# Neighbourhood attention on one core: mask set-up issued earlier, ScalarE's last stores issued one per tick, a border wait undeclared, and matmuls added to the last step

## The chip, the cores and the metric

The kernel runs on one NeuronCore of a Trainium2 chip. The metric is the device time of one execution in microseconds, smaller is better. The engines are TensorE (PE, with its weight loads as PEld), VectorE (DVE), ScalarE (ACT), GpSimd (POOL) and SyncE (SP). Each has its own instruction stream and runs it in order. SP only issues DMAs here. ACT and POOL issue DMAs too, between their other instructions.

## The reference

The image is 224 x 224 with 192 channels. Each pixel attends to 49 pixels: a 7 x 7 window of dilation 2, shifted inwards at the image's edges.

```
qkv = x @ wqkv                       # q, k, v: 224 x 224 x 192 each
r0 = clip(row - 6, 0, 211); c0 = clip(col - 6, 0, 211)
neighbours of a pixel: rows r0 + 0,2,..,12 and columns c0 + 0,2,..,12
logits = (q . k_neighbour) * 192**-0.5
o = softmax(logits) @ v_neighbours
out = o @ wo
```

All inputs are bfloat16.

## The kernel before, in words

Dilation 2 splits the image by row parity `rc` and column parity `cc`; within one parity the window is a dense 7 x 7. The queries are never formed as such: `aw` holds scale * wq * wk^T, so that `pg` = x * aw is compared with the raw image rows (the keys are copies of `x`), and `WP` holds wv * wo, so that `vw` = x * WP is already the projected value. A column of ones in `vw` gives the softmax's denominator.

The work is a list of 28 **steps** `(rc, j)`: (0,0), (1,1), (0,1), (1,2), ..., (1,13), (1,14), (0,13). A step is a strip of query rows of one row parity. It has 7 **ticks** (`i` from 6 down to 0); a tick handles four blocks of keys:

- `s_stage`: PE computes scores into one of two banks (`s_83`, `s_84`, L428), ACT writes their exponentials to `p_sb` (L431).
- `attend`, two ticks later: `v_stage` multiplies `p_sb` with `vw` into two accumulating banks (`y_85`, `y_86`, L448). `out_stage` takes a finished bank: DVE's reciprocal `rs` (L502) and product `o_sb` (L503), then stores (`store`, L466 and L468). In step (1,14) the products go to `oall` and leave in strided stores too (L515).
- Between them, units of the next step's work: `pv` = keys * WP (L279), evicted to `vw` by DVE and ACT in halves (L290); `pg` = keys * aw (L368), evicted by ACT to `ga`, or to `hs`, which POOL copies to `gb` (L385). `edge_item` and `place_edges` do the same for the image's left and right border (`pe`, `ge`, L347). POOL copies key blocks for the step after next (`make_keys`, L254).

The score's mask is part of the matmul. Free rows of the key tiles `xb` hold one-hot patterns (`onehot_cols`, `onehot_rows`, L164 and L170), and the same rows of the query tiles `gb` hold mask values (`mask_cols`, `mask_rows`, L149 and L154). DVE makes `xb_90`'s and `gb_102`'s; the other buffers get theirs partly from POOL and partly by SBUF-to-SBUF DMAs on SP (`spread_masks`, `spread_onehots`, L159 and L179). In buffer numbers of the profile, `XB[0..3]` are `xb_90` to `xb_93` and `GB[0..5]` are `gb_98` to `gb_103`.

The **border tile**: in the first tick of each step the last key block also reaches 6 image columns beyond the accumulators. Their sums go to `T.border`, 48 partitions in the second bank of the `pv` tile whose first bank holds a `vw` unit (`spare`). DVE's reciprocal `rse` (L487) and product `oe` (L489) read it. The instructions that evict the `vw` unit, DVE's and ACT's, are passed along as `readers`.

`load_xt` (L71) fetches a strip of the image with a transposing DMA on SP. `o_sb` has six buffers for the single tiles and two for the double tile of tick `i == 0`. Instructions run on each engine in the order in which the code emits them; waits come from tile dependencies, which are kept per buffer.

Of the kernel before, what the change touches and what calls it, by code (L numbers as in the profile page):

```python
# [31 lines left out]
def kernel(  # L32
# [147 lines left out]

    onehot_cols(0, nc.vector.tensor_copy)
# [7 lines left out]
    def warm(n):  # L189

        for _ in range(n):
            nc.tensor.matmul(y_bank[1][:].rearrange("p c e -> p (c e)"), lhsT=zero[:, 0:128], rhs=zero[:], start=True, stop=True,  # L192
                             skip_group_check=True)
# [206 lines left out]
    class Tick:  # L400
        border = None

# [31 lines left out]
    def v_stage(T, spare):  # L434


        for pos, (cc, n) in enumerate(T.pos):
# [3 lines left out]
            if not (cc == 0 and n == NT - 1):  # L441
                h, sl = 64 * ((n + 1) % 2), ((n + 1) // 2) % 2
                if n == NT - 1:
                    tile_, readers = spare or (ps_go.tile([128, 2, 2, 256], F32, name="pv", tag="go"), [])
                    T.border = tile_[0:48, 1, 0, 0:C + 1]
                parts.insert(0, (T.p[:, pos, 64:112], T.border if n == NT - 1 else y_bank[sl][h:h + 48, cc, 0:C + 1], n == NT - 1))
            for (l, o, st) in parts:
                mm = nc.tensor.matmul(o, lhsT=l, rhs=rhs, start=st, stop=True, skip_group_check=True)  # L448
# [23 lines left out]
    qn = [0]  # L472

    def out_stage(T):
# [10 lines left out]
        if i == NQ - 1:  # L485
            rs = work.tile([48, 1], F32, name="rse", tag="rse", bufs=2)
            nc.vector.reciprocal(out=rs[:], in_=T.border[:, C:C + 1])  # L487
# [11 lines left out]
        for t in range(t0, t1):  # L499
# [8 lines left out]
            if t == 0:  # L508
                for p in pieces:
                    store(pick(nc.sync), lambda d: op[d, 3:13, :], of, 6, 16, p)  # L510
                    store(pick(nc.gpsimd), lambda d: oc[d, 0:6, :], o[:, t - t0, 0], 0, 6, p)
        if last and i in (0, NQ // 2):
            ta, tb = (1, NQ // 2 + 1) if i == 0 else (NQ // 2 + 1, NQ)
            for (r0, _, d0, _) in pieces:
                pick(None).dma_start(out=op[d0, 16 * ta - 3:16 * tb - 3, :].rearrange("(t c) e -> c t e", c=16),  # L515
                                     in_=oall[r0::8, ta:tb].rearrange("p n t c -> p n (t c)"))
# [18 lines left out]
    onehot_rows(1, nc.gpsimd.tensor_copy)  # L535
# [4 lines left out]
    load_xt(2)  # L540
    both = (nc.vector, nc.gpsimd)
# [10 lines left out]
    for si, (rc, j) in enumerate(steps):  # L552
# [10 lines left out]
        for ti, i in enumerate(range(NQ - 1, -1, -1)):  # L563
# [12 lines left out]
            if si == 0 and ti == 0:  # L576
                mask_rows(3, 2, nc.gpsimd.tensor_copy)
# [66 lines left out]
```

## Time and profile before

| what | value |
|---|---|
| time, median of 3 runs | 348.85 us (348.04 to 350.31) |
| profiled execution | 346.11 us, its span 344.3 us |
| mean granted clock of TensorE | 0.967 |
| busy: PE, PEld | 303.1 us (88%), 275.6 us (80%) |
| busy: DVE, ACT, POOL | 263.9 us (77%), 253.3 us (74%), 236.3 us (69%) |
| DMA | 43.79 MB, mean 127 GB/s |

The span runs from the first to the last instruction of the profiled execution; 1.8 us of that execution lie outside it. No engine is busy throughout, so the shares do not name a bound. The view of idle time by releaser (who waited for whom) and the chain of work that ended last do that, stage by stage.

### The profile page before, as it was taken

The numbers are of one execution on the slowest core, as the hardware profiler recorded it, in microseconds if no ns is written. First come the engines' busy times: TensorE is split into PE (matmuls) and PEld (weight loads), VectorE is DVE, ScalarE is ACT, GpSimd is POOL, SyncE is SP. The second block draws the span as 40 slices with busy tenths as digits, with TensorE's granted clock in tenths as the row PEclk, the third lists the DMA queues.
The fourth block names the chain that finished last, engine by engine and source line by source line (L and its number), as shares of the span: only waits on it lengthen the run. The fifth ranks groups of instructions, "written<-read, shape, count | busy, mean of one in ns | idle before, by whom it ended". The sixth has DMA issues, their size and how long they took to land.

```text
span 344.3 us, 17618 instructions
## 1 busy us (share of the span) xinstructions
PE 303.1 (88%) x7488; PEld 275.6 (80%) x7488; DVE 263.9 (77%) x609; ACT 253.3 (74%) x424; POOL 236.3 (69%) x501
## 2 busy tenths in 40 slices
PE   7876797699999998999999999998998999988853
PEld 2455697688999997899998889897998899887842
DVE  7636987478887887878888778886787877888733
ACT  4335776677888877888888888887887888778820
POOL 5444539956997775977767977678775787861960
PEclk9688999999999999999999999999999999999976
DMA  8971445984949668294663847539385294222123
GB/s 195 208 166 33 102 119 131 169 203 109 183 113 160 149 145 155 73 187 118 111 166 90 188 106 162 131 77 199 89 187 102 74 186 118 64 78 53 46 55 86
DMA packets 112409, 43.79 MB, mean 127 GB/s; under 512 B 86984, under 2 KB 111874, under 8 KB 112330
## 3 DMA queue, kind: packets, MB, share of 16 engines
q1 hardware_dynamic: 109370, 41.00, 55.2%
q0 software_dynamic: 2368, 1.35, 2.0%
q8 instruction: 58, 0.95, 1.2%
q10 hardware_dynamic: 592, 0.31, 0.4%
q14 instruction: 21, 0.17, 0.2%
HBM read 0.29 MB, written 19.35 MB: 57 GB/s over the span
## 4 chain that ended last, share of the span: by engine, by line
PE 55%; DVE 23%; issue 9%; ACT 6%; DMA 3%; POOL 1%; ACTq 1%; SPq 0%; DVEq 0%; POOLq 0%
PE pv L279 14%; PE y_85 L448 11%; PE pg L368 10%; DVE o_sb L503 9%; DVE vw L290 6%; PE y_86 L448 5%; PE s_83 L428 5%; PE s_84 L428 4%; DMA out_dram<-o_sb 3%; DVE rs L502 3%; PE y_86 L192 2%; ACT p_sb L431 2%; ACT vw L290 2%; PE pe L322 2%; ACT hs L372 1%
## 5 line engine op out<-in xcount | busy, mean ns | idle before, releaser
L290 DVE CAST vw<-pv 64x768 bf16<-64x768 f32 (+1 forms) x112 | 95.6, 854 | 12.3 <-PE pv L279 5.2
L448 PEld LDWEIGHTS <-p_sb 128*64 128x64 bf16 (+1 forms) x1540 | 79.1, 107 | 25.7 <-issue 22.3
L290 ACT CAST vw<-pv 64x768 bf16<-64x768 f32 (+1 forms) x112 | 79.7, 712 | 27.0 <-PE pv L279 20.3
L448 PE MATMUL y_85<-vw,p_sb 128*64 128x193 bf16 (+1 forms) x840 | 85.9, 249 | 12.6 <-DVE o_sb L503 9.7
L448 PE MATMUL y_86<-vw,p_sb 128*64 128x193 bf16 (+1 forms) x672 | 82.3, 252 | 3.8 <-DVE o_sb L503 2.5
L368 PE MATMUL pg<-xt,aw 128*64 128x106 bf16 (+3 forms) x1008 | 81.6, 289 | 2.6 <-DVE vw L290 1.5
L503 DVE TENSOR_TENSOR o_sb<-y_85,rs 128x384 bf16<-128x384 f32 x108 | 60.2, 558 | 4.6 <-DMA out_dram<-o_sb 0.9
L431 ACT ACTIVATE p_sb<-s_84 128x448 bf16<-128x448 f32 x98 | 53.5, 546 | 7.3 <-DMA out_dram<-oall 5.6
L431 ACT ACTIVATE p_sb<-s_83 128x448 bf16<-128x448 f32 x98 | 53.6, 547 | 5.3 <-PE s_83 L428 4.3
L368 PEld LDWEIGHTS <-aw 128*64 128x64 bf16 x1008 | 52.5, 111 | 5.6 <-DVE vw L290 1.9
L466 POOL DMA_DIRECT2D out_dram<-o_sb x26 | 15.0, 578 | 60.4 <-DVE rs L502 60.4
L428 PEld LDWEIGHTS <-xa_87 128*64 128x64 bf16 x532 | 46.6, 112 | 4.6 <-issue 3.9
L503 DVE TENSOR_TENSOR o_sb<-y_86,rs 128x384 bf16<-128x384 f32 x81 | 45.1, 557 | 6.1 <-DMA out_dram<-o_sb 3.4
L428 PEld LDWEIGHTS <-xa_88 128*64 128x64 bf16 x532 | 47.4, 111 | 1.1 <-issue 0.6
L428 PEld LDWEIGHTS <-xa_89 128*64 128x64 bf16 x476 | 41.6, 110 | 0.4
L428 PEld LDWEIGHTS <-xb_90 128*64 128x64 bf16 x420 | 34.2, 113 | 2.4 <-issue 1.9
L428 PEld LDWEIGHTS <-xb_91 128*64 128x64 bf16 x420 | 35.3, 112 | 0.2
L502 DVE RECIPROCAL rs<-y_86 128x2 f32<-128x2 f32 x84 | 14.0, 167 | 25.7 <-PE y_86 L448 25.7
L372 ACT CAST hs<-pg 128x848 bf16<-128x848 f32 x27 | 23.4, 866 | 11.5 <-PE pg L368 10.6
L279 PE MATMUL pv<-WP,xa_87 128*64 128x192 bf16 x280 | 30.0, 253 | 1.6 <-ACT vw L285 0.5
L428 PEld LDWEIGHTS <-xb_92 128*64 128x64 bf16 x364 | 29.7, 110 | 0.5
L279 PE MATMUL pv<-WP,xa_88 128*64 128x192 bf16 x280 | 28.5, 247 | 1.0 <-DVE vw L290 0.5
(169 smaller groups left out, 1020.4 us busy)
## 6 DMA issues: line engine op xcount, KB each, us to landing
out_dram<-o_sb SPq DMA_DIRECT2D x162, 96.0 KB
out_dram<-o_sb SPq DMA_DIRECT2D x27, 60.0 KB
out_dram<-oe POOLq DMA_DIRECT2D x26, 18.0 KB, 2.7
out_dram<-o_sb POOLq DMA_DIRECT2D x26, 18.0 KB, 3.1
xb_92<-xb_90 SPq DMA_DIRECT2D x4, 112.0 KB
xb_93<-xb_91 SPq DMA_DIRECT2D x4, 112.0 KB
out_dram<-oall POOLq DMA_DIRECT2D x9, 36.0 KB, 1.8
xt<-in_x_dram SPq DMA_TRANSPOSE x15
```

Of the source, the lines that this page charges most:

```text
L192: nc.tensor.matmul(y_bank[1][:].rearrange("p c e -> p (c e)"), lhsT=zero[:, 0:128], rhs=zero[:], start=True, stop=True, skip_group_check=True)
L279: nc.tensor.matmul(pv[h:h + 64, (n - n0) // 2, (n - n0) % 2, 0:C], lhsT=keys(k, rc, cc, kt)[:, n, :], rhs=WP[:, cc, kt, :], start=(kt == 0 ...
L290: ins.append(eng(out=VW[hs, rc, cc, n0:n1, 0:C], in_=pv[hs].rearrange("p a b c -> p (a b) c")[:, 0:n1 - n0, 0:C]))
L322: nc.tensor.matmul(pg[64 * h:64 * h + 64, g // 2, g % 2, par], lhsT=AW[w][:, 64 * h:64 * h + 64], rhs=r, start=(i == 0), stop=(i == 1))
L368: nc.tensor.matmul(pr[64 * h:64 * h + 64, g, a_ - 4 * g:b_ - 4 * g, :], lhsT=AW[w][:, 64 * h:64 * h + 64], rhs=xt[b][:, k, l, 3:S - 3], st ...
L372: return eng(out=dst[:, 6:S].rearrange("p s (g r) -> p s g r", r=4), in_=pr[ps].rearrange("p g r s -> p s g r"))
L428: nc.tensor.matmul(o[h:h + 64, s0:s1, rs], lhsT=keys(k, rc, cc, kt)[:, n, :], rhs=(A, Bt)[kt][:, cc, CW * n + s0:CW * n + s1, rs], start=( ...
L431: nc.scalar.activation(out=T.p[:].rearrange("p a b -> p (a b)"), in_=ps[:, 0:4 * QW * BR], func=ACTF.Exp)
L448: mm = nc.tensor.matmul(o, lhsT=l, rhs=rhs, start=st, stop=True, skip_group_check=True)
L466: q.dma_start(out=dst, in_=src[8 * s0:8 * s1])
L502: nc.vector.reciprocal(out=rs[:], in_=y[:, :, C:C + 1])
L503: nc.vector.tensor_tensor(out=o[:, t - t0], in0=y[:, :, 0:C], in1=rs[:].to_broadcast([128, 2, C]), op=ALU.mult)
```

## The change

Four things change.

1. **Prologue and first steps.** POOL's `mask_rows(3, 2)`, `mask_rows(2, 1)` and `onehot_rows(1)` are emitted before DVE's part of the masks, ahead of everything else POOL does after its iotas. The spreads that steps 0 and 1 issued on SP between the stores are issued after the third image load. `load_xt(3)` is issued in the first tick of step 1 and not in the third.
2. **ACT's late stores.** A store that falls to ACT while ticks are still pending goes into `held`; one is taken from it at the end of each tick.
3. **The border tile.** The readers of the other bank were declared independent of the border's matmul already. Now DVE's reciprocal and product on the border are declared independent of `readers[1:]`, which is ACT's eviction.
4. **The last step.** Two matmuls of 128 x 512 on zeros follow each of its seven ticks, into a tile of the `go` pool.

```diff
+    mask_rows(3, 2, nc.gpsimd.tensor_copy)
+    mask_rows(2, 1, nc.gpsimd.tensor_copy)
+    onehot_rows(1, nc.gpsimd.tensor_copy)
     onehot_cols(0, nc.vector.tensor_copy)
     onehot_rows(0, nc.vector.tensor_copy)
     mask_cols(4, nc.vector.tensor_copy)
...
-    def warm(n):
+    def warm(n, bank=None):
+        bank = bank or y_bank[1][:].rearrange("p c e -> p (c e)")
         for _ in range(n):
-            nc.tensor.matmul(y_bank[1][:].rearrange("p c e -> p (c e)"), lhsT=zero[:, 0:128], rhs=zero[:], start=True, stop=True,
-                             skip_group_check=True)
+            nc.tensor.matmul(bank, lhsT=zero[:, 0:128], rhs=zero[:], start=True, stop=True, skip_group_check=True)
...
     class Tick:
         border = None
+        readers = ()
+
+        def apart(self, op, first=0):
+            for rd in self.readers[first:]:
+                tc.declare_no_dep(op.ins, rd.ins, reason="they are in the other bank of the tile")
...
                 if o is T.border:
-                    for rd in readers:
-                        tc.declare_no_dep(mm.ins, rd.ins, reason="they are in the other bank of the tile")
+                    T.apart(mm)
...
+    held = []
+
+    def put_off(q, issue, *args):
+
+        if q is nc.scalar and pend:
+            held.append(lambda: issue(q, *args))
+        else:
+            issue(q, *args)
...
-            nc.vector.reciprocal(out=rs[:], in_=T.border[:, C:C + 1])
+            T.apart(nc.vector.reciprocal(out=rs[:], in_=T.border[:, C:C + 1]), 1)
...
-            nc.vector.tensor_tensor(out=o[:], in0=T.border[:, 0:C], in1=rs[:].to_broadcast([48, C]), op=ALU.mult)
+            T.apart(nc.vector.tensor_tensor(out=o[:], in0=T.border[:, 0:C], in1=rs[:].to_broadcast([48, C]), op=ALU.mult), 1)
             for p in pieces:
-                store(pick(nc.gpsimd), lambda d: oc[d, W - 6:W, :], o, 0, 6, p)
+                put_off(pick(nc.gpsimd), store, lambda d: oc[d, W - 6:W, :], o, 0, 6, p)
...
     load_xt(2)
+    spread_masks(1, 3, 64)
+    spread_onehots(2)
+    spread_masks(2, 4, 32)
+    spread_onehots(3)
+    spread_masks(0, 2, 64)
+    spread_masks(5, 4, 32)
...
             if si == 0 and ti == 3:
                 make_keys(1, 0, *both)
-                spread_masks(1, 3, 64)
-                spread_masks(2, 4, 32)
-                spread_onehots(2)
-                spread_onehots(3)
-                mask_rows(2, 1, nc.gpsimd.tensor_copy)
-            if si == 1 and ti == 1:
-                spread_masks(0, 2, 64)
-                spread_masks(5, 4, 32)
...
-            if si == 1 and ti == 2 or si > 1 and rc == 0 and ti == 0:
+            if ti == 0 and (si == 1 or si > 1 and rc == 0):
                 load_xt(j + 2 + (rc == 0))
             pend.append(T)
+            if held:
+                held.pop(0)()
+            if si == len(steps) - 1:
+                warm(2, ps_go.tile([128, 512], F32, name="idle", tag="go")[:])
         assert not v_q and not q_q, (si, len(v_q), len(q_q))
-    attend(1)
-    attend(1)
+    while pend:
+        attend(1)
+    while held:
+        held.pop(0)()
```

The other stores of `out_stage` go through `put_off` in the same way. On DVE and on PE up to the last step the order of instructions is the same; of the waits there, the reciprocal `rse` loses the one for ACT. Three places move.

**POOL in the prologue.** In the program before, after the last iota, POOL clears two parts of `WP`, sets the ones of `vw`, places the first edges (eight rows, two shown) and then makes the one-hot rows and mask rows of step 1.

```order
L137 IOTA rwi 32x2
L229 MEMSET WP 64x192
L230 MEMSET WP 64x192
L245 MEMSET vw 128x14 x4
L347 COPY ga_95<-ge 128x6x7
L347 COPY gb_102<-ge 64x6x7
```

After the change, at the same place:

```order
L137 IOTA rwi 32x2
L154 COPY gb_101<-rm 32x944 x2
L154 COPY gb_100<-rm 32x944 x2
L170 COPY xb_91<-t_r 32x896 x2
L232 MEMSET WP 64x192
L233 MEMSET WP 64x192
L248 MEMSET vw 128x14 x4
L350 COPY ga_95<-ge 128x6x7
```

Six copies have moved ahead of the memsets and the edges; they stand no longer behind the edges (four of them) or behind the key copies of tick 3 (the two on `gb_100`).

**SP in steps 0 and 1.** Before, the spreads stand behind stores of step 0, and the last four stand behind all of them, just ahead of the fourth image load:

```order
L466 DMA out_dram<-o_sb 16x8x384
L468 DMA out_dram<-o_sb 16x384
L159 DMA gb_98<-gb_100 64x944 x2
L159 DMA gb_103<-gb_102 32x944 x2
L71 DMA_TRANSPOSE xt<-in_x_dram 128x3x1792
L466 DMA out_dram<-o_sb 16x8x384 x5
L71 DMA_TRANSPOSE xt<-in_x_dram 128x3x1792
```

After, the piece between the third and the fourth image load begins with all sixteen spreads and no store; the fourth load then stands ahead of the last four stores of step 0:

```order
L71 DMA_TRANSPOSE xt<-in_x_dram 128x3x1792
L159 DMA gb_99<-gb_101 64x944 x2
L179 DMA xb_92<-xb_90 64x896 x4
L159 DMA gb_100<-gb_102 32x944 x2
L179 DMA xb_93<-xb_91 64x896 x4
L159 DMA gb_98<-gb_100 64x944 x2
L159 DMA gb_103<-gb_102 32x944 x2
L473 DMA out_dram<-o_sb 16x8x384
L475 DMA out_dram<-o_sb 16x384
```

**ACT in the last step.** Before, four stores of step (1,14) stand between the exponentials of its second and third tick:

```order
L431 ACTIVATE p_sb<-s_83 128x448
L468 DMA out_dram<-oall 10x384
L468 DMA out_dram<-oall 6x192
L468 DMA out_dram<-oall 10x384
L515 DMA out_dram<-oall 16x3x384
L431 ACTIVATE p_sb<-s_84 128x448
L466 DMA out_dram<-oe 6x8x192
L431 ACTIVATE p_sb<-s_83 128x448
```

After, each exponential is followed by one store:

```order
L439 ACTIVATE p_sb<-s_83 128x448
L475 DMA out_dram<-oall 10x384
L439 ACTIVATE p_sb<-s_84 128x448
L475 DMA out_dram<-oall 6x192
L439 ACTIVATE p_sb<-s_83 128x448
L475 DMA out_dram<-oall 10x384
L439 ACTIVATE p_sb<-s_84 128x448
L530 DMA out_dram<-oall 16x3x384
L439 ACTIVATE p_sb<-s_83 128x448
L473 DMA out_dram<-oe 6x8x192
```

One store, not four, stands ahead of the third exponential.

More of the change, by code (lines that the diff above doesn't have):

```diff
@@ L443, in v_stage @@
                 if n == NT - 1:
-                    tile_, readers = spare or (ps_go.tile([128, 2, 2, 256], F32, name="pv", tag="go"), [])
+                    tile_, T.readers = spare or (ps_go.tile([128, 2, 2, 256], F32, name="pv", tag="go"), [])
                     T.border = tile_[0:48, 1, 0, 0:C + 1]
@@ L514, in out_stage @@
             for (r0, _, d0, _) in pieces:
-                pick(None).dma_start(out=op[d0, 16 * ta - 3:16 * tb - 3, :].rearrange("(t c) e -> c t e", c=16),
-                                     in_=oall[r0::8, ta:tb].rearrange("p n t c -> p n (t c)"))
+                put_off(pick(None), lambda q, ta, tb, r0, d0: q.dma_start(
+                    out=op[d0, 16 * ta - 3:16 * tb - 3, :].rearrange("(t c) e -> c t e", c=16),
+                    in_=oall[r0::8, ta:tb].rearrange("p n t c -> p n (t c)")), ta, tb, r0, d0)
     steps = [(0, 0)]
```

6 lines of the change are left out of this document (2 added, 4 removed).

## The prediction

> **What bounds the kernel now.** I read the page first for the span, then the view of idle time by releaser, and then the timeline and the table of stretches at the places where a part of the change bites. From the waits:
>
> ```profile
> span 344.3 us, 17618 instructions
> PE y_85 L448 <- DVE o_sb L503: 9.7, 28, 0.8
> DVE rse L487 <- ACT vw L290: 7.4, 14, 0.7
> ACT p_sb L431 <- DMA out_dram<-oall: 5.6, 1, 5.6
> DVE o_sb L503 <- DMA out_dram<-o_sb: 4.3, 4, 2.2
> PE s_84 L428 <- ACT p_sb L431: 3.5, 1, 3.5
> ```
>
> Columns: total us, times, longest. No engine is the bound alone. PE and DVE wait for one another: PE may not add to a y bank until DVE has read it, DVE may not read until PE has finished it. A delay on DVE inside that loop is paid by PE. Three of these rows are delays that come from outside the loop: DVE waits for ACT at the border (7.4 us), DVE waits for stores to leave its buffers (4.3 us), and ACT's exponential waits behind stores (5.6 us, of which PE feels 3.5). The change touches each.
>
> **The change part by part**
>
> *Border wait.* One instance, in the timeline:
>
> ```profile
> 115.64 0.54 DVE L290 CAST vw<-pv 64x384 bf16<-64x384 f32 x1
> 116.24 0.47 ACT L290 CAST vw<-pv 64x384 bf16<-64x384 f32 x1
> 116.74 0.16 DVE L487 RECIPROCAL rse<-pv 48x1 f32<-48x1 f32 x1 [0.56 <-ACT vw L290]
> 118.01 0.24 PE L448 MATMUL y_85<-vw,p_sb 128*64 128x193 bf16 x1 [0.43 <-DVE o_sb L503]
> ...
> 62.91 0.24 PE L448 MATMUL y_85<-vw,p_sb 128*64 128x193 bf16 x1 [0.43 <-DVE o_sb L503]
> ...
> 288.02 0.24 PE L448 MATMUL y_85<-vw,p_sb 128*64 128x193 bf16 x1 [0.42 <-DVE o_sb L503]
> ```
>
> DVE ends its own eviction at 116.18 and stands 0.56 us until ACT has evicted the other half, of a bank that the border isn't in. The product that frees y_85 follows, and PE sits 0.43 us for it. The last two rows are the first and the last of twelve such places, all with 0.42 to 0.44 us (steps 2, 3, 6, 7, 10, 11, 14, 15, 18, 19, 22, 23); elsewhere DVE comes to the border late anyway. The reciprocal keeps its wait for PE, which had written the border by then (the PE row ends 1 us earlier). So 0.56 us of DVE goes and PE gets its 0.43 us; what PE does next (the `pv` unit) finds its buffers free. 12 x 0.425 = **5.1 us**. Bounds: 0, if something else is late there by as much, and 14 x 0.53 = 7.4 us, DVE's whole idle time.
>
> *Spreads and the fourth load on SP.*
>
> ```profile
> 19.85 5.46 SPq L71 DMA_TRANSPOSE xt<-in_x_dram  x1
> ...
> 53.93 1.17 SPq L159 DMA_DIRECT2D gb_98<-gb_100  x2
> 56.42 6.69 SPq L71 DMA_TRANSPOSE xt<-in_x_dram  x1
> 63.21 3.65 SPq L466 DMA_DIRECT2D out_dram<-o_sb  x5
> 66.95 5.42 SPq L71 DMA_TRANSPOSE xt<-in_x_dram  x1
> ...
> 65.58 0.56 DVE L503 TENSOR_TENSOR o_sb<-y_86,rs 128x384 bf16<-128x384 f32 x1 [2.19 <-DMA out_dram<-o_sb]
> ...
> 61.65:74.58 12.93, 10.07 (x265) 9.44 (x261) 8.25 (x20) 8.95 (x15) 8.82 (x18) 1.00 0.85 194
> 74.58:85.30 10.72, 9.93 (x259) 9.17 (x255) 8.47 (x20) 8.72 (x14) 7.57 (x17) 1.00 0.43 110
> 106.59:116.74 10.15, 9.69 (x265) 9.37 (x261) 8.35 (x20) 8.95 (x15) 7.97 (x17) 1.00 0.99 180
> 116.74:126.76 10.02, 9.56 (x258) 9.06 (x254) 8.64 (x21) 8.70 (x14) 7.58 (x17) 1.00 0.45 111
> ```
>
> SP issues in order, and an image load holds it 5.4 to 6.7 us. Two loads stand within 16 us here, with step 1's five stores between them; the stores are issued only from 63.2 on, and DVE runs out of its six `o_sb` buffers. The stretches from border to border show what that costs: 12.93 and 10.72 us, where the same two kinds of step (same numbers of instructions) later take 10.15 and 10.02: 2.78 + 0.70 = 3.48 us. Afterwards the sixteen spreads, 0.6 us each by the row at 53.93, stand behind the third load, at about 25.3 to 35.5, where SP issued nothing before. By the same 0.6 us per store I estimate the rest: load four starts about 47.6, behind the store of step 0's fifth single tile, and ends near 54.3; the four stores of step 0's last tile and step 1's five leave by 60, where load five begins. The stores behind it leave from 66.6 on; the earliest buffer needed again belongs to the store at about 68, is back by 71 and wanted at about 73. So the stall goes: **3.5 us**, bounds 0 (the load just stalls other stores) and 4.3 (the wait's own row).
>
> *POOL's copies in the prologue.* This costs.
>
> ```profile
> 9.44 0.81 DVE L154 COPY gb_102<-rm 32x944 bf16<-32x944 bf16 x2
> 12.71 0.36 DVE L325 CAST ge<-pe 128x192 bf16<-128x192 f32 x1 [2.46 <-PE pe L322]
> 14.14 1.04 DVE L372 CAST gb_102<-pg 64x848 bf16<-64x848 f32 x1 [0.24 <-PE pg L368]
> 15.22 0.40 DVE L254 COPY xa_87<-xt 128x896 bf16<-128x896 bf16 x1
> 15.29 2.14 POOL L170 COPY xb_91<-t_r 32x896 bf16<-32x896 bf16 x2
> 15.53 1.12 DVE L254 COPY xb_90<-xt 64x896 bf16<-64x896 bf16 x1
> ...
> 13.40 0.22 POOL L347 COPY ga_95<-ge 128x42 bf16<-128x42 bf16 x1 [7.80 <-ACT ge L326]
> ```
>
> POOL idles 7.8 us before its first edge, and the six copies (three pairs like the one at 15.29, 2.14 us) fill 6.4 of them. But DVE makes its own eight mask copies in that time, the last two ending at 10.25, and where a copy of DVE meets one of POOL (15.53), it took 1.12 us and not 0.40: it waited 0.72 us. Six POOL copies can hold up six DVE copies so, 4.4 us; DVE has 2.46 us before its edge cast and 0.24 more before its next eviction, so at most 1.7 us reach the first score matmul. If POOL's own gaps let part of them through, nothing does. I take **0.8 us lost**, the middle, since the one row is of the same kind of copy. The places that the copies leave bring nothing by themselves, since POOL idles soon after both.
>
> The Trainium skill, page "SBUF — State Buffer", section "Who interferes with whom", says that a VectorE copy in a two-port mode and a GpSimd instruction exclude each other for a whole instruction. The row at 15.53 agrees; by the rule all eight copies of DVE are exposed, and an estimate by it would lie near the 1.7 us end, which makes the sum 8.4 and not 9.3.
>
> *ACT's late stores.*
>
> ```profile
> 328.25 3.21 ACTq L468 DMA_DIRECT2D out_dram<-oall  x3
> 331.55 0.71 ACTq L515 DMA_DIRECT2D out_dram<-oall  x1
> 332.37 0.54 ACT L431 ACTIVATE p_sb<-s_84 128x448 bf16<-128x448 f32 x1 [5.60 <-DMA out_dram<-oall]
> ...
> 328.24 5.36 SPq L468 DMA_DIRECT2D out_dram<-oall  x7
> 333.71 1.89 SPq L515 DMA_DIRECT2D out_dram<-oall  x3
> 335.70 5.95 SPq L466 DMA_DIRECT2D out_dram<-o_sb  x7
> ...
> 340.10 0.56 DVE L503 TENSOR_TENSOR o_sb<-y_86,rs 128x384 bf16<-128x384 f32 x1
> ...
> L466 SPq DMA_DIRECT2D out_dram<-o_sb x189: 537/550/1869, 35.1 to 340.9; - x189
> DMA to landing us min/median/max: 1.9/3.0/7.7
> ```
>
> With one store and not four ahead of the exponential of 332.37, it starts about 3 us sooner (3.21 + 0.71 less one share of 1.07), and DVE's last product ends near 337.7 instead of 340.66. But SP is late next: its ten stores of step (1,14) still run from 328.24 to 335.6, and the seven tile stores follow, at 0.55 us each (median) to 0.73 (3.65 / 5 above). The last issue ends at 339.6 to 340.8 and not at 341.65: 0.9 to 2.1 us. I take **1.5 us**. The held stores cost ACT some 0.3 us per tick, and that fits under SP.
>
> *Matmuls in the last step.* After the 3.5 us gap PE ran at half its clock:
>
> ```profile
> 332.90:337.00 4.10, 4.04 (x73) 3.90 (x73) 1.76 (x6) 2.14 (x5) 0.68 (x2) 0.50 0.27 75
> 10.01 1.89 PE L192 MATMUL y_86<-zero 128*128 128x512 bf16 x4
> ```
>
> Without the gap it stays faster. Two more matmuls per tick are 0.9 us of PE by the second row (clock 0.80), against ticks of 1.3 us (the first row holds about three) in which PE's own work is about 0.7 at full clock (4.04 at half clock, by three). An overshoot of 0.3 us in seven ticks, 2.1 us, would bring DVE's end to 339.8, level with SP: **0**, at worst 0.5 lost.
>
> Sum: 5.1 + 3.5 - 0.8 + 1.5 = **9.3 us** less. The profiled execution, 346.11 us (344.3 and 1.8 around it), would become 336.8. That execution was 2.7 us quicker than the median of the runs, 348.85; I take the difference from the median: **339.5 us**. A difference under 1% (3.5 us) can hardly be told from none on this kernel.
>
> **The rivals**
>
> *The border gain is absorbed.* ACT idles only 0.6 us before its next eviction, and its own chain could set the step once DVE's is shorter; then half or all of the 5.1 us stay. Against: at 118.01 PE waited for nothing but DVE. With all of it gone: 348.85 - 4.2 = 344.7.
>
> *The early load only moves the stall.* 6.7 us of SP stand ahead of step 0's last four stores, of which the double tile has two buffers. Then 3.5 goes: 343.0. Against: load five then starts behind cleared stores, not 0.1 us after them.
>
> *ACT's held stores block its exponentials.* They go through the hardware queues together with SP's, and each waits until an earlier transfer of its lane has landed, as the program's semaphores have it. If that holds ACT for a median landing, 3.0 us, at each of four stores, ACT ends 12 us later and, less 1.6 us of slack under SP, the tail loses 10.4 instead of gaining 1.5: 351.4, slower than before. It outweighs the other 7.8 us from 2.4 us a store upwards. For it: the three stores of L468 took 1.07 us each. Against: SP's own, with the same waits, go at 0.6 to 0.8.
>
> *Nothing that counts.* The dropped wait is taken over by PE and the stall returns in step 3; prologue loss and tail gain cancel: 347.
>
> **How the numbers follow.** Forecast 0.60; border absorbed 0.15 (half of it still over 1%); stall moved 0.12; nothing 0.07; held stores block 0.06. Faster 0.60 + 0.08 + 0.12 = 0.80, same 0.07 + 0.07 = 0.14, slower 0.06. The best terms (5.6 for the border with two more places, 4.3, no loss, 2.1) make 12 us less, 336.9; from the lowest run shown, 348.04, 336.0. Upwards the range takes in both absorbed cases, to 345. So 336 to 345.
>
> **What would show it.** In the profile after: the row of the reciprocal waiting for ACT gone, PE's wait for `o_sb` shorter by about 5 us, and steps 6 and 7 each 0.4 us shorter (right or wrong on the border); no wait of `o_sb` for a store between 60 and 85; DVE's mask copies in 6 to 15 us longer than now, and the first score matmul at 18.2 to 19.4 instead of 17.77; ACT's exponentials of the last step about 1.3 us apart and SP issuing tile stores back to back at the end. Wrong: steps of unchanged length with a new releaser before `rs` or `y_85`, or ACT waiting for landings in the last step.

## The result, and the profile after

The changed kernel takes **338.42 us** (median; 337.26 to 339.05) where the kernel before, run beside it, takes 348.47 (348.04 to 350.31): a ratio of **0.970, 95% interval 0.965 to 0.974**. The prediction was 339.5 us, in 336 to 345. On the second of the three chips used further down, five of the eleven executions of the kernel before took over 1.5% longer than its fastest there, and they are left out of its median and of the ratios.

The profiled execution took 338.49 us, with a span of 336.4. Its idle time by releaser (total us, times, longest):

```profile
span 336.4 us, 17622 instructions
PE y_85 L456 <- DVE o_sb L518: 4.0, 16, 0.8
PE pg L371 <- ACT ge L329: 3.2, 1, 3.2
DVE o_sb L518 <- DMA out_dram<-o_sb: 2.5, 2, 2.0
ACT p_sb L439 <- PE y_85 L456: 2.9, 2, 2.6
```

The reciprocal's wait for ACT (7.4 us before) is gone, and PE's wait for the product that frees y_85 has fallen from 9.7 to 4.0 us. The row of ACT waiting for stores (5.6 us) is gone too. Over half of DVE's wait for stores is still there (2.5 of 4.3 us), and a wait is new: PE stands 3.2 us for the edge eviction, in the prologue.

The table of stretches, at the places that answer to those of before (start:end in us, length, busy time of PE, weight loads, DVE, ACT and POOL with counts, granted clock, DMA share, GB/s):

```profile
61.80:71.37 9.57, 9.54 (x266) 9.35 (x262) 8.26 (x22) 8.96 (x15) 8.87 (x19) 1.00 0.96 185
71.37:83.41 12.04, 10.64 (x273) 9.73 (x269) 8.46 (x22) 9.32 (x16) 8.24 (x17) 1.00 0.47 118
104.19:113.76 9.57, 9.54 (x266) 9.34 (x262) 8.27 (x21) 8.96 (x15) 7.99 (x17) 1.00 0.94 190
113.76:123.84 10.08, 10.05 (x273) 9.68 (x269) 8.66 (x22) 9.29 (x16) 8.25 (x17) 1.00 0.48 120
```

These run from the border reciprocal of step 2, 3, 6 and 7 to that of the next step. They were 12.93, 10.72, 10.15 and 10.02 us. The border edit shows in the third: PE is busy for 9.54 of 9.57 us. In the second there are now 12.04 us: a wait for stores that was in step 2 has come to step 3.

In the prologue (DVE first, POOL below):

```profile
6.29 2.23 DVE L164 COPY xb_90<-t_c 32x896 bf16<-32x896 bf16 x2
8.53 2.58 DVE L170 COPY xb_90<-t_r 32x896 bf16<-32x896 bf16 x2
11.13 1.97 DVE L149 COPY gb_102<-cm 32x944 bf16<-32x944 bf16 x2
13.13 1.12 DVE L154 COPY gb_102<-rm 32x944 bf16<-32x944 bf16 x2
14.28 0.36 DVE L328 CAST ge<-pe 128x192 bf16<-128x192 f32 x1
5.21 1.98 POOL L154 COPY gb_101<-rm 32x944 bf16<-32x944 bf16 x2 [0.49 <-DVE rm L141]
9.40 2.49 POOL L170 COPY xb_91<-t_r 32x896 bf16<-32x896 bf16 x2
11.95 0.65 POOL L232 MEMSET WP<- 64x192 bf16 x1
```

DVE's eight mask copies end at 14.25 and not 10.25, and the edge cast follows at 14.28 with no wait for PE, where it had waited 2.46 us and started at 12.71.

And the last step, SP, ACT and DVE:

```profile
321.07 5.37 SPq L475 DMA_DIRECT2D out_dram<-oall  x7
326.54 2.02 SPq L530 DMA_DIRECT2D out_dram<-oall  x3
328.66 5.07 SPq L473 DMA_DIRECT2D out_dram<-o_sb  x7
321.07 1.60 ACTq L475 DMA_DIRECT2D out_dram<-oall  x1
322.78 0.54 ACT L439 ACTIVATE p_sb<-s_84 128x448 bf16<-128x448 f32 x1 [2.60 <-PE y_85 L456]
323.62 0.54 ACT L439 ACTIVATE p_sb<-s_83 128x448 bf16<-128x448 f32 x1 [0.29 <-PE idle L196]
330.13 0.56 DVE L518 TENSOR_TENSOR o_sb<-y_86,rs 128x384 bf16<-128x384 f32 x1
```

DVE's last product ends at 330.69, but SP issues until 333.73, and the span ends 2.7 us behind that. The exponential at 322.78 still stands behind a store: the one ahead of it takes until 322.67 to issue. The view names PE as the releaser, but PE's last matmul into `s_84` starts at 321.04 and the ones into y_85 behind it end by 321.6. So ACT's wait has shrunk from four stores to one.

**Where the time went.** I cut the span at the border reciprocals, one per step, whose start times the timeline gives; up to the last border all kernels have the same work between them. In us:

| kernel | start to step 0's border | step 0 | step 1 | steps 2, 3 | steps 4 to 26 | last border to end | span |
|---|---|---|---|---|---|---|---|
| before | 29.80 | 19.64 | 12.21 | 23.65 | 243.50 | 15.50 | 344.3 |
| before_again | 27.09 | 19.60 | 12.21 | 25.01 | 244.71 | 15.38 | 344.0 |
| after | 31.88 | 18.33 | 11.59 | 21.61 | 238.22 | 14.77 | 336.4 |
| after_again | 31.89 | 18.32 | 11.60 | 19.99 | 239.13 | 14.77 | 335.7 |
| border_alone | 29.83 | 19.36 | 11.59 | 25.58 | 242.47 | 15.47 | 344.3 |
| pool_late | 29.76 | 19.66 | 11.59 | 20.61 | 239.56 | 14.82 | 336.0 |
| load_old | 31.73 | 19.26 | 11.61 | 20.37 | 241.09 | 14.74 | 338.8 |
| spreads_old | 31.39 | 18.31 | 11.61 | 24.83 | 240.29 | 14.57 | 341.0 |
| osb8 | 32.70 | 18.32 | 11.59 | 19.64 | 240.13 | 14.82 | 337.2 |
| tail_pool | 31.21 | 18.32 | 11.59 | 20.13 | 240.01 | 17.04 | 338.3 |
| no_hold | 31.34 | 18.33 | 11.60 | 19.96 | 237.08 | 16.59 | 334.9 |
| tail_act | 31.41 | 18.32 | 11.61 | 20.28 | 241.39 | 12.89 | 335.9 |
| no_warm | 31.39 | 19.68 | 11.61 | 20.26 | 240.17 | 14.99 | 338.1 |
| pool_late_tail_act | 32.07 | 18.32 | 11.59 | 20.72 | 240.69 | 12.91 | 336.3 |

The kernels from border_alone on are the experiments below. Among kernels with the same edit there, step 1 repeats to a few hundredths and the end to 0.25 us. The other columns move by one to five us from run to run, so an edit is judged in the column that it touches, and most columns of a kernel rest on a single profile.

From the first to the third row: +2.08, -1.31, -0.62, -2.04, -5.28, -0.73; in all -7.9 us. The medians differ by 10.05.

### The profile page after: what moved, and what is told of

Its sections match the earlier page's. It is cut to its first block, busy times and chain, and to the rows that moved or that the text cites. A ratio compares the mean times of both kernels' runs of the same rounds, so it can differ in the third digit from the quotient of the medians.

```text
span 336.4 us, 17622 instructions
## 1 busy us (share of the span) xinstructions
PE 301.5 (90%) x7502; PEld 273.3 (81%) x7502; DVE 266.4 (79%) x609; ACT 253.3 (75%) x424; POOL 238.6 (71%) x501
## 4 chain that ended last, share of the span: by engine, by line
PE 62%; DVE 23%; issue 7%; POOL 2%; ACT 2%; DMA 1%; SPq 0%; DVEq 0%; POOLq 0%; ACTq 0%
PE pv L282 16%; PE pg L371 13%; PE y_85 L456 11%; DVE o_sb L518 8%; DVE vw L293 7%; PE s_83 L436 7%; PE s_84 L436 6%; PE y_86 L456 6%; DVE rs L517 2%; PE pe L325 2%; DMA out_dram<-o_sb 1%; PE idle L196 1%; DVE vw L288 1%; DVE xb_90 L170 1%; DVE xb_90 L164 1%
## 5 line engine op out<-in xcount | busy, mean ns | idle before, releaser
L456 PE MATMUL y_85<-vw,p_sb 128*64 128x193 bf16 (+1 forms) x840 | 84.9, 246 | 6.3 <-DVE o_sb L518 4.0
L456 PEld LDWEIGHTS <-p_sb 128*64 128x64 bf16 (+1 forms) x1540 | 77.1, 106 | 16.0 <-issue 12.0
L456 PE MATMUL y_86<-vw,p_sb 128*64 128x193 bf16 (+1 forms) x672 | 78.9, 248 | 1.5 <-issue 1.1
L371 PEld LDWEIGHTS <-aw 128*64 128x64 bf16 x1008 | 53.2, 110 | 7.9 <-issue 3.7
L436 PEld LDWEIGHTS <-xa_88 128*64 128x64 bf16 x532 | 46.1, 110 | 3.6 <-issue 3.1
L436 PEld LDWEIGHTS <-xa_87 128*64 128x64 bf16 x532 | 45.5, 111 | 0.8
L436 PEld LDWEIGHTS <-xa_89 128*64 128x64 bf16 x476 | 41.0, 110 | 0.4
L436 PEld LDWEIGHTS <-xb_90 128*64 128x64 bf16 x420 | 33.2, 111 | 1.8 <-issue 1.3
L436 PEld LDWEIGHTS <-xb_91 128*64 128x64 bf16 x420 | 34.2, 110 | 0.2
L282 PE MATMUL pv<-WP,xa_87 128*64 128x192 bf16 x280 | 30.7, 256 | 1.5 <-issue 0.5
L436 PEld LDWEIGHTS <-xb_92 128*64 128x64 bf16 x364 | 29.4, 110 | 0.5
L282 PE MATMUL pv<-WP,xa_88 128*64 128x192 bf16 x280 | 28.5, 246 | 1.0 <-DVE vw L293 0.5
```

Of the source, the lines that this page charges most:

```text
L282: nc.tensor.matmul(pv[h:h + 64, (n - n0) // 2, (n - n0) % 2, 0:C], lhsT=keys(k, rc, cc, kt)[:, n, :], rhs=WP[:, cc, kt, :], start=(kt == 0 ...
L371: nc.tensor.matmul(pr[64 * h:64 * h + 64, g, a_ - 4 * g:b_ - 4 * g, :], lhsT=AW[w][:, 64 * h:64 * h + 64], rhs=xt[b][:, k, l, 3:S - 3], st ...
L436: nc.tensor.matmul(o[h:h + 64, s0:s1, rs], lhsT=keys(k, rc, cc, kt)[:, n, :], rhs=(A, Bt)[kt][:, cc, CW * n + s0:CW * n + s1, rs], start=( ...
```

## The experiments

Four of them were run on one chip, four on a second, four on a third; the kernel before had a median of 351.3, 347.8 and 350.3 us there. Ratios are to the kernel before on the same chip.

### The border wait alone

The kernel before with this edit only:

```
+            T.apart(nc.vector.reciprocal(out=rs[:], in_=T.border[:, C:C + 1]), 1)
...
+            T.apart(nc.vector.tensor_tensor(out=o[:], in0=T.border[:, 0:C], ...), 1)
```

> The kernel before with one edit of the change alone: reciprocal and product of the border no longer wait for ACT's eviction from the tile's other bank. Theory A (DVE's 0.56 us per border was paid by PE at twelve to fourteen borders, and nothing else is late there): steps 4 to 27 take 5.3 us less (243.5 to 238.2), the two steps ahead of them 0.9 less, prologue and last step are unchanged; 6.2 us less in all, 342.3 us beside 348.5. Rival (ACT's own chain takes the wait over, and the gain needs the other edits): half of it or less, 345.5 or more. In the profile by A the reciprocal waits for ACT nowhere and the stretch from step 6's border to step 7's falls from 10.15 to 9.6 us.

Measured: 344.97 us, ratio 0.979 (0.974 to 0.984), so 5.6 to 9.3 us less. The edit needs none of the others. Its profile is less clean than theory A had it: its span of 344.3 us is no shorter than the first one of the kernel before. Step 1's stretch falls to 11.59 as it does in the changed kernel, but steps 2 and 3 get longer (25.58):

```profile
DVE o_sb L507 <- DMA out_dram<-o_sb: 4.7, 1, 4.7
PE s L433 <- issue: 4.6, 3, 2.1
```

One wait of 4.7 us stands there; I take it that the faster steps reach the blocked buffers earlier, but the kernel before has a wait of 3.8 us in one piece in its second profile. The second row is PE standing still with no releaser that the profile shows; those gaps come in every kernel (last section), and one of them, 1.0 us, lies in step 6, which took 10.59 and not the 9.6 expected. In the undisturbed step 10 the stretch fell from 10.15 to 9.50. Of the nine stretches in front of the other places that the prediction names, steps 2 and 6 left out, eight fell by 0.48 to 0.65 us and one (step 18) by 0.04.

### POOL's copies behind the edges

```
-    mask_rows(3, 2, nc.gpsimd.tensor_copy)
-    mask_rows(2, 1, nc.gpsimd.tensor_copy)
-    onehot_rows(1, nc.gpsimd.tensor_copy)
     onehot_cols(0, nc.vector.tensor_copy)
...
     spread_masks(3, 4, 32)
+    onehot_rows(1, nc.gpsimd.tensor_copy)
...
             if si == 0 and ti == 0:
+                mask_rows(3, 2, nc.gpsimd.tensor_copy)
                 make_keys(0, 1, nc.vector, nc.vector)
                 make_keys(1, 1, *both)
+                mask_rows(2, 1, nc.gpsimd.tensor_copy)
+                spread_masks(1, 3, 64)
+                spread_onehots(2)
+                ...
```

> The changed kernel with POOL's three pairs of mask copies no longer ahead of its edge copies in the prologue, but where they stood before, in and behind it (the row masks of GB 3 and GB 2 in the first tick), and the spreads that need them issued there too, still at the same place in SP's queue. Theory A (the copies hold up DVE's eight mask copies for whole instructions, which moves the first score matmul by 1.6 us and keeps PE at half clock for longer): DVE's mask copies end at 10.3 and not 14.25, the first score matmul goes back to 17.8, the first border reciprocal comes at 29.8 and not 31.9; of these 2.1 us 1.3 are lost again in step 0, whose start falls into the lower clock, so 0.8 us net: 337.6. Rival B (the clock is no matter of when PE starts, and the whole 2.1 us stay): 336.3. Rival C (behind the first tick the copies hold up POOL's key copies, and DVE by its lock, as long as they did in the prologue): 338.4 or more.

Measured: 337.74 us, ratio 0.959 (0.954 to 0.964). DVE's side of its prologue:

```profile
9.46 0.81 DVE L154 COPY gb<-rm 32x944 bf16<-32x944 bf16 x2
12.70 0.36 DVE L325 CAST ge<-pe 128x192 bf16<-128x192 f32 x1 [2.43 <-PE pe L322]
```

The mask copies end at 10.27 again, and the first border comes at 29.76, the second 19.66 later: 49.42 us, where the changed kernel has 31.88 + 18.33 = 50.21. In this pair that is theory A to a tenth: the copies cost 2.1 us in the prologue, 1.3 of which come back in step 0, 0.8 net (pool_late_tail_act, further down, doesn't repeat it). What comes back is the clock:

```profile
29.80:49.44 19.64, 16.73 (x372) 14.49 (x369) 15.78 (x31) 13.76 (x24) 9.40 (x18) 0.91 0.37 88
31.88:50.21 18.33, 15.37 (x372) 13.50 (x369) 15.79 (x32) 13.65 (x24) 7.49 (x16) 1.00 0.34 80
```

(before, then after): with the same 372 matmuls PE is busy 1.36 us less, at a granted clock of 1.00 and not 0.91. In load_old and no_warm below, which keep the early copies, step 0 took 19.26 and 19.68 at a granted clock of 0.91 again, in spite of the late start (31.73 and 31.39). So this return is not certain, and what decides it is not shown. The ratio is lower than the changed kernel's 0.970 (0.972 on the second chip) by more than 0.8 us explains; the two weren't run on one chip, so I rest on the columns.

### The fourth load, and the spreads, back at their old places

```
-            if ti == 0 and (si == 1 or si > 1 and rc == 0):
+            if si == 1 and ti == 2 or si > 1 and rc == 0 and ti == 0:
                 load_xt(j + 2 + (rc == 0))
```

> The changed kernel with load four where it was, in the third tick of step 1; the spreads stay behind load three. Theory A (the stall of o_sb in steps 2 and 3 is made by how close loads four and five stand, so the place of load four carries the gain): load four starts at 53 to 54 and not 49.9, step 1's five stores fall between two loads again, and the stretches of steps 2 and 3 grow by 1.2 us: 339.6. Rival B (taking sixteen spreads, 10 us of SP, out of step 0's and step 1's stores carries the gain; the load is only moved past four stores and load five stays at about 64): within 0.4 us of the changed kernel, 338.4.

```
     load_xt(2)
-    spread_masks(1, 3, 64)
-    ...
             if si == 0 and ti == 3:
                 make_keys(1, 0, *both)
+                spread_masks(1, 3, 64)
+                ...
+            if si == 1 and ti == 1:
+                spread_masks(0, 2, 64)
+                spread_masks(5, 4, 32)
```

> The changed kernel with the sixteen spreads where they were (twelve in step 0's fourth tick, four in step 1's second), load four staying in the first tick of step 1. Theory A (the spreads between step 0's stores carry the gain): step 0's stores leave late again, load four starts at 50 to 51, load five at 66 to 67 behind four more spreads, steps 1 to 3 take some 1.8 us longer: 340.2. Rival B (the place of load four carries it): 338.4 to 338.8, load four at 50 and the o_sb stall no longer than the 2.5 us it has in the changed kernel.

Measured on one chip: with the load at its old place 339.42 us, ratio 0.966 (0.962 to 0.970); with the spreads at theirs 343.11 us, ratio 0.975 (0.970 to 0.979). SP in load_old, then DVE in spreads_old:

```profile
53.08 5.43 SPq L71 DMA_TRANSPOSE xt<-in_x_dram  x1
58.62 3.68 SPq L473 DMA_DIRECT2D out_dram<-o_sb  x5
62.39 5.51 SPq L71 DMA_TRANSPOSE xt<-in_x_dram  x1
...
67.04 0.56 DVE L518 TENSOR_TENSOR o_sb<-y,rs 128x384 bf16<-128x384 f32 x1 [3.94 <-DMA out_dram<-o_sb]
```

In load_old the two loads stand 3.9 us apart, as near as they stood before (3.8), and DVE waits for no store at all; steps 2 and 3 take 20.37. In spreads_old load four starts at 51.72, 4.7 us sooner than before, and DVE waits 3.94 us in one piece; steps 2 and 3 take 24.83. Slow loads are no rival here, since both kernels had quick ones (5.43 and 5.51 us, 5.81 and 5.55). So the spreads carry the term; a share of the load's place is not to be seen beside the spread of these columns (19.6 to 21.6 us in all profiles with early spreads). Theory A of the first falls; of the second it holds, with 4 us in these steps and not 1.8.

### Two more buffers

```
-            o = work.tile([128, nt, 2, C], BF, name="o_sb", ..., bufs=6 if nt == 1 else 2)
+            o = work.tile([128, nt, 2, C], BF, name="o_sb", ..., bufs=8 if nt == 1 else 2)
```

The changed kernel was run on the same chip:

> The changed kernel as it is, for comparison on one chip with the three beside it. Both theories: 0.97 of the kernel before; its profile again shows PE stretches in the prologue and steps as in the first one (first border reciprocal at 31.9, about 2.5 us of o_sb waiting for stores in step 3, SP's last issue 12.1 us after the last border reciprocal).

> The changed kernel with eight buffers for the single o_sb tiles and not six. Theory A (what is left of the stall is DVE running out of buffers while a load holds SP): two more buffers are two more ticks, 2.8 us, more than the 2.5 us that are left; the row of o_sb waiting for stores goes, step 3 falls from 12.04 to 10.1, and the time is 2 us (0.6%) below the changed kernel of the same chip. Rival B (SP issues more than it can keep up with, so the buffers only put the wait off): the wait comes back in step 5 behind the next load, and the time is the same within 0.5 us.

Measured: 338.01 us against 337.93 for the changed kernel: no difference. The wait of o_sb for stores is gone, step 3 takes 10.07 us, and no such wait comes back later (step 5 takes 9.80 and 9.95 in the changed kernel). But the changed kernel had only 0.8 us of that wait here, not 2.5, so 0.35 us was all there was to gain in steps 2 and 3 (19.99 to 19.64). The six other profiles whose step 2 takes 9.57 us all have such a wait, of 0.7 to 2.5 us, so the buffers seem to cure it; they settle nothing on the time.

```profile
49.18 5.58 SPq L71 DMA_TRANSPOSE xt<-in_x_dram  x1
62.82 5.79 SPq L71 DMA_TRANSPOSE xt<-in_x_dram  x1
```

This is SP in after_again. In the first profile of the changed kernel the same two loads took a microsecond longer each:

```profile
49.94 6.59 SPq L71 DMA_TRANSPOSE xt<-in_x_dram  x1
63.86 6.67 SPq L71 DMA_TRANSPOSE xt<-in_x_dram  x1
```

The 2.5 us of that profile go with two slow loads, but the other profiles don't make a rule of it: tail_act's loads took 5.59 and 5.64 us and o_sb waited 1.15 us, no_warm's took 5.86 and 6.69 and it waited for nothing. What sets the rest of the stall stays open.

### The end of the program

Three of the last seven tile stores to POOL; ACT's late stores not held; three of the seven to ACT; no matmuls on zeros:

```
-                    store(nc.sync, lambda d: op[d, 16 * t - 3:16 * t + 13, :], of, 0, 16, p)
+                    store(nc.gpsimd if (rc, j) == steps[-1] and t % 2 else nc.sync, ...)    # tail_pool
+                    store(nc.scalar if (rc, j) == steps[-1] and t < 4 else nc.sync, ...)    # tail_act
...
-        if q is nc.scalar and pend:
+        if False:                                                                           # no_hold
...
-            if si == len(steps) - 1:
-                warm(2, ps_go.tile([128, 512], F32, name="idle", tag="go")[:])              # no_warm
```

> The changed kernel with three of the seven tile stores of the last step issued by POOL and not by SP. Theory A (SP's queue sets the end: after its ten stores of the ring's step it has seven tile stores of 0.72 us, while DVE's last product ends 3 us before SP's last issue): SP issues four behind 328.6 and is through at 331.5, some 0.8 us behind DVE's last product; 2.1 us less than the changed kernel of the same chip. Rival B (the transfers themselves set the end, or a store issued by POOL lands that much later): within 0.5 us of the changed kernel.

> The changed kernel with ACT's late stores issued at once, as before (four ahead of the first exponential that needs ACT); the matmuls in the last step stay. Theory A (ACT's gap costs what DVE's end moves behind SP's): DVE's last product comes 11.9 us behind the last border reciprocal, SP's last issue about 12.9 behind it instead of 12.1; 0.7 to 0.8 us more than the changed kernel of the same chip. Rival B (with PE kept busy the gap no longer halves the clock, and the ticks catch up under SP): within 0.3 us of it. Rival C (the held stores brought the whole 3 us of ACT's wait): 2 us more or above.

> The changed kernel with the last three of the last step's seven tile stores (tiles 3, 2 and 1) issued by ACT, whose last exponential ends some 3.4 us ahead of DVE's last product, and not by SP. Theory A (SP's last issue sets the end: in each profile so far of kernels that end with SP the span ended 2.6 to 2.7 us behind it): SP and ACT are both through at 9.9 us behind the last border reciprocal instead of 12.1, and the stretch from that reciprocal to the end is 12.6 us and not 14.8. Rival B (the transfers set the end, so that with more issuers each takes longer to land): 14.3 us or more. Rival C (a store on ACT waits for the landing of earlier ones of its lane, 2 to 3 us each): 14 to 16 us.

> The changed kernel without the two idle matmuls per tick in the last step. Theory A (SP sets the end and DVE's last product has 2.3 us to spare ahead of it): the stretch from the last border reciprocal to the end stays at 14.8 us, within 0.3; DVE's last product comes 9.1 us behind that reciprocal or up to 1 us earlier, since PE has 1.08 us less per tick. Rival B (without them PE's clock halves in the last step): DVE's last product comes 11 us or more behind it and the stretch grows to 16 or more.

Measured on the second chip (the changed kernel 337.93 us): tail_pool **340.23**, no_hold **339.46**. On the third: tail_act **337.61**, ratio 0.962 (0.958 to 0.967), and no_warm **339.33**, ratio 0.969 (0.965 to 0.974).

*tail_act*: the last border to the end is 12.89 us instead of 14.77.

```profile
329.49 3.35 ACTq L473 DMA_DIRECT2D out_dram<-o_sb  x4
330.04 2.77 SPq L473 DMA_DIRECT2D out_dram<-o_sb  x4
331.51 0.56 DVE L518 TENSOR_TENSOR o_sb<-y,rs 128x384 bf16<-128x384 f32 x1
```

Both queues are through 0.8 us behind DVE's last product (332.07), and the span ends 3.1 us later. This is theory A: SP's last issue set the end of the changed kernel.

*tail_pool* relieves SP in the same way, and yet loses 2.3 us:

```profile
330.62 0.53 POOL L473 DMA_DIRECT2D out_dram<-o_sb  x1 [2.61 <-DVE o_sb L518]
...
332.00:334.00 2.00, 0.00 (x0) 0.00 (x0) 0.00 (x0) 0.00 (x0) 0.00 (x0) 0.50 0.18 54
334.00:336.00 2.00, 0.00 (x0) 0.00 (x0) 0.00 (x0) 0.00 (x0) 0.00 (x0) 0.50 0.00 0
336.00:338.30 2.30, 0.00 (x0) 0.00 (x0) 0.00 (x0) 0.00 (x0) 0.00 (x0) 0.50 0.00 0
```

SP is through at 331.06 and POOL at 331.15. The DMA engines stop moving data before 334, and the span ends at 338.3, 7.15 us behind POOL's last issue. Neither theory gives this price: A had 2.1 us less, rival B the same time within 0.5 us. Nor was a transfer late: POOL's three tile stores landed in 2.1 us by the median. Something that follows a store from POOL at the end of the program takes the time; what it is, the profile doesn't show.

*no_hold*: the end takes 16.59 us. ACT's exponential waits for four stores in a row, as before:

```profile
317.76 3.13 ACTq L475 DMA_DIRECT2D out_dram<-oall  x3
318.20 0.60 PE L196 MATMUL idle<-zero 128*128 128x512 bf16 x2
320.99 0.72 ACTq L530 DMA_DIRECT2D out_dram<-oall  x1
321.81 0.55 ACT L439 ACTIVATE p_sb<-s 128x448 bf16<-128x448 f32 x1 [4.94 <-DMA out_dram<-oall]
325.17 1.03 PE L196 MATMUL idle<-zero 128*128 128x512 bf16 x2
```

DVE's last product comes 12.9 us behind the last border (331.18), where it came 9.1 behind in the changed kernel and 11.9 (340.66) in the one before. The price, 1.8 us in this column and 1.5 in the medians, lies between theories A and C. The kernel before has the same gap without the idle matmuls, and an end of 15.4 to 15.5 us: so the matmuls, slower behind the gap (1.03 us for two, which took 0.60 ahead of it; granted clock 0.63 from 325 to 328), make the late ticks about 1 us later still, past SP.

*no_warm*: the end takes 14.99 us, 0.2 more. PE's clock in the last step, without those matmuls:

```profile
323.11:331.00 7.89, 4.42 (x108) 3.28 (x102) 4.71 (x16) 2.72 (x5) 4.79 (x10) 1.00 0.19 52
```

It stays at 1.00. DVE's last product ends 8.6 us behind the border, 0.4 sooner than with them, and SP's issues end 12.3 behind it. So they bring nothing that shows in the kernel as changed, and hide behind SP. That is theory A.

### Both reasons together, and the kernel before again

The changed kernel with the edits of pool_late and tail_act, and the kernel before once more:

> The changed kernel with POOL's mask copies behind its edge copies, and tiles 3 to 1 of the last step stored by ACT. Theory A (both reasons hold, and they touch different ends): first border reciprocal at 29.8 and second at 49.4 (50.2 in the changed kernel), last stretch 12.6: 3.0 us below the changed kernel, about 0.962 of the kernel before. Rival (the prologue's gain is lost in the stores' wait of steps 2 and 3, as the earlier steps demand the buffers earlier): 2.2 us below it.

> The kernel before once more, for a second profile of it: its first profiled run took 346.1 us beside a median of 348.5 to 351.3. Theory A (its runs differ by how long o_sb waits for stores in steps 2 to 5, since loads and stores share SP there): prologue, step 0 and last step agree with the first profile within 0.2 us, and steps 2 to 5 differ by one to five. Rival B (single gaps of PE of 1 to 2 us with no releaser, which come at other places in each run): the steps differ, and o_sb waits 4 to 5 us again.

Measured: pool_late_tail_act **336.35 us**, ratio **0.961 (0.956 to 0.965)**, the lowest median of all, against 337.61 for tail_act on the same chip; the intervals of the two overlap. Its end is 12.91 us, as expected, but its first border came at 32.07 and not 29.8. before_again took 345.75 us, with the first border at 27.09. The five profiles with DVE's mask copies free of POOL's have it at 27.1, three times at 29.8, and at 32.1 us, then. The edge cast in before_again and in pool_late_tail_act, and ahead of each a matmul of the weight product that it needs:

```profile
8.29 0.27 PE L220 MATMUL prA<-wT_lo 128*64 128x192 bf16 x1
10.65 0.36 DVE L325 CAST ge<-pe 128x192 bf16<-128x192 f32 x1 [0.39 <-PE pe L322]
...
10.43 0.37 PE L220 MATMUL prA<-wT_lo 128*64 128x192 bf16 x1
14.27 0.36 DVE L325 CAST ge<-pe 128x192 bf16<-128x192 f32 x1 [4.00 <-PE pe L322]
```

The same matmul takes 0.27 us in one run and 0.37 in the other, and comes 2.1 us later: PE's speed in the first ten us differs between runs, and there PE sets the edge cast, DVE waiting 0.4 to 4.0 us. It looks like the clock, but the table of stretches gives a granted clock of 1.00 for 5 to 10 us in both, so that is not shown. In every kernel with the early copies the cast stands at 14.27 to 14.41, since there DVE's own copies set it (in osb8 PE, by 0.17 us). So the 0.8 us of the copies is their price against a prologue like the first; against before_again's it is 50.21 - 46.69 = 3.5 us, against pool_late_tail_act's none (50.39). On the mean of the five profiles without the early copies (49.03 to step 1's border) and of the nine with them (50.24) it is 1.2 us, but the five range from 46.69 to 50.39, so the size of the price stays open.

The o_sb wait of before_again is 3.8 us, its steps 2 and 3 take 25.01 and 1.4 us more than in the first profile, step 4 another 1.4: so the steps are theory A's, the wait is near theory B's amount, and A's claim on the prologue is wrong by 2.7 us.

## Why the prediction was right, and where its terms were off

The time came out 1.1 us from the forecast, through the mechanisms of the forecast, with sizes that were partly luck.

*Border wait* (5.1 us expected). Right in mechanism, too small in size. The gain stands in the stretches in front of the twelve places named: ten of the twelve lost 0.51 to 0.71 us, one (step 14) 0.06, and step 2's can't be read beside the stores. That is 6.2 us in eleven. I had said that steps 6 and 7 would each get shorter; step 6 did (10.15 to 9.57), step 7, which ends at none of these places, didn't (10.02 to 10.08). I had counted PE's 0.43 us per place; what came back was DVE's whole 0.56, and PE's wait of 9.7 us fell by 5.7. The rival that ACT takes the wait over is out: border_alone shows the gain without the other edits.

*Spreads and load* (3.5 us). The size held on the mean, the reason given was half wrong. I put the stall down to two loads within 16 us with five stores between them. load_old has the two loads as near, and no stall; what counts is the 10 us of spreads that stood among the stores of steps 0 and 1. The times that I had worked out for SP were too early as well: load four started at 49.94 and not about 47.6, load five at 63.86 and not 60, and so o_sb did wait for stores between 60 and 85 (1.96 us at 75.10), which I had ruled out. The rival "the early load only moves the stall" looked half right in the first profile, where 2.5 us of the wait had moved to step 3 and only about 1.5 us were gained there beyond the border's share. The other nine profiles of kernels with early spreads have 19.6 to 20.7 us in steps 2 and 3, the four without 23.1 to 25.6 (the two before less 0.57 for the border): 4.1 us between the means of all ten and of the four.

*POOL's copies* (0.8 lost). 0.77 in the first pair of profiles, and pool_late returns just that. But the way there was another. The first score matmul came 1.59 us late (19.36 after 17.77), just inside my bound of 1.7, and the first border 2.1 us, since not six but all eight mask copies of DVE were held up (7.90 us in the four rows of the profile after, 0.78 + 1.27 + 1.31 + 0.81 = 4.17 before), the last two by POOL's memsets, which stood behind the copies and took 0.65 us each instead of 0.25 in the kernel before. I had counted the POOL copies and left out what was queued behind them. The clock then gave 1.3 us back in step 0 of that pair, which I hadn't seen; that the two came to my 0.8 was luck. The Trainium skill, page "SBUF — State Buffer", section "Who interferes with whom", says that the engine that issues first holds the shared ports for a whole instruction; the estimate by it, which I set beside my own, was the better one for the prologue, and DVE's row at 8.53 (1.29 us a copy, where it took 0.64) agrees with it.

*ACT's late stores* (1.5, from 0.9 to 2.1). Right that SP is late next; 0.73 came, below my lower bound. The term that failed is the rate of SP's tile stores: the seven took 5.07 us, 0.72 each, the upper of the two rates that I had, and not the median 0.55; and the ten stores ahead of them ended 0.1 us later than before. SP's last issue stands 12.10 us behind the last border, before 12.85. The rival that held stores block the exponentials is out (the first took 1.60 us, the four behind it 0.67 to 0.75, and the exponentials from 322.78 on stand 0.8 to 1.3 us apart). Without the hold the changed kernel would be 1.5 to 1.8 us worse, since it carries the idle matmuls.

*Matmuls in the last step* (0). Confirmed by no_warm, within 0.2 us, and so is what I said of the clock: without the gap it stays at 1.00, with the matmuls or without. Their price was too high. I took 0.9 us for two from the row at 10.01 and read its clock as 0.80; the granted clock from 10.01 to 11.90 is 0.50. In the last step two take 0.60 us, and DVE's last product comes 0.4 us later for them, not 2.1.

A slip of the sums besides: the rival without any gain was put at 347, but its terms cancel, which leaves 348 to 349.

The columns of the first pair of profiles make 7.9 us, the forecast 9.3, the medians 10.05. Both profiles of the kernel before are quicker than most of its timed runs (346.1 and 345.75 us beside medians of 348.5 and 350.3), while those of the changed kernel stand at its median. So some 2 us of the gain lie in executions that no profile shows. That the spans' varying parts, stall and prologue clock, make them is likely and not shown.

## What to carry to other kernels

Price a stall in a queue by everything that stands in the queue ahead of the late work, not by the largest item: taking 10 us of small copies out from between the stores did what moving the large load didn't. Before filling an engine's idle time, list what is queued behind the filling, and ask whether a neighbour that it holds up is on the path there (DVE's eight copies took 7.90 us beside POOL's, not 4.17). Where one queue's last issue sets the end, give part of its issues to a queue that is idle by then, but test which: ACT's gained 1.9 us, POOL's lost 2.3.

## What the runs showed of the hardware that was not expected

- A store issued from POOL as the last thing cost 7.15 us from its issue to the end of the span, 4.3 of them with no DMA traffic; one from SP or ACT 2.7 to 3.1 us.
- PE stands still for 1 to 2 us with no releaser shown, each time soon after an image load has been issued: in the fourteen profiles 50 such gaps of 0.9 us or more begin 1.1 to 3.1 us behind the end of a load's issue. In border_alone:

```profile
85.11 5.94 SPq L71 DMA_TRANSPOSE xt<-in_x_dram  x1
94.62 0.24 PE L433 MATMUL s<-gb,xb 128*64 128x112 bf16 x1 [2.08 <-issue]
128.33 5.56 SPq L71 DMA_TRANSPOSE xt<-in_x_dram  x1
136.91 0.21 PE L433 MATMUL s<-gb,xb 128*64 128x64 bf16 x2 [1.52 <-issue]
```

  The gaps begin at 92.54 and 135.39, 1.5 us behind the loads' ends at 91.05 and 133.89. In load_old the gap that ends at 90.40 is 1.26 us, in the first profile of the changed kernel the one that ends at 129.47 is 0.98. They help to move the column of steps 4 to 26 by several us between runs: no_hold, the lowest, has one of them there, the others two to five. No run tried their cause.
- What a late start costs depends on the clock as much as on the delay: in the first pair the first border came 2.1 us late and the second 0.8, with a granted clock of 1.00 and not 0.91 between them (load_old and no_warm started late and had 0.91 all the same); and the kernel before itself reached the first border at 29.8 in one profile and 27.1 in another.
